# One core, a transformer block with a spectral filter, forward and backward: row stores and filter gradients issued by GpSimd, a column move on VectorE, four row statistics on ScalarE, and the queues written out anew

## The chip, the core and the metric

The kernel runs on one core of a Trainium2 chip. The core has five engines with a queue each: TensorE (PE in the profile; its weight loads are shown apart as PEld), VectorE (DVE), ScalarE (ACT), GpSimd (POOL) and SyncE (SP, which here only starts transfers). The metric is the time of one execution on the device in microseconds; the number given for a kernel is the median of its runs.

## The reference, cut to what matters

Inputs are bf16: x of 1x2048x512, a spectral filter w_r + i w_i of 2048x257, an MLP of width 1792 (w1, b1, w2, b2), a condition c of 1x512 and its matrix w_mod of 512x3072.

```python
def forward(x, w_r, w_i, w1, b1, w2, b2, c, w_mod):
    sa, ca, ga, sb, cb, gb = split6(silu(c) @ w_mod)
    h = layernorm(x) * (1 + ca) + sa
    x = x + ga * irfft2(rfft2(h) * (w_r + 1j * w_i))
    h = layernorm(x) * (1 + cb) + sb
    r = maximum(h @ w1 + b1, 0)
    return x + gb * ((r * r) @ w2 + b2)
```

The kernel returns this output (out_0) and, for a given grad_out, the gradients of all nine inputs: x (out_1), w_r and w_i (out_2, out_3), w1, b1, w2, b2 (out_4 to out_7), c (out_8) and w_mod (out_9).

## The kernel before, in words

**Tiling.** The 2048 rows lie as 16 tiles (NT) of 128 rows by 512 columns. The MLP takes them in four batches (NB) of four tiles, so 512 rows, and its 1792 columns in 14 pieces of 128 (NFC). The two-dimensional transforms are products with tables: the first stage over rows (spec_f1_half, "f1"), then for eight groups gi the second and third (spec_f23, "f2" and "f3"); spec_g1 and "g2", "g3" are the way to the other side. The backward pass runs through the same functions with the filter conjugated; it is called the way back here.

**Stages, in order of time.** (1) To about 15 us: the first loads; products of ones with themselves that nobody reads (L760, the warm-up products); silu(c); products with w_mod, among them column products mod_cols (L802) for gb2x, the factor 2 gb; transposes of w2, copied with that factor into w2T (L819); transposes of the first rows of grad_out into gT. (2) To about 47 us: statistics, norm and f1 for pairs of tiles (row_stats, row_norm), and the back products of the MLP, back_products (L912): for each batch and each of 14 pieces four products w2T x gT in one PSUM bank, copied to gaT by VectorE (one in five) or ScalarE. The banks of these products are the two buffers of "mm". In this stage the rest of the rows of mod (L789) and the bias row of the transform (psd, L891) are computed, too. (3) To about 79 us: the way there, spec_f23 then spec_g1. In spec_f23 one psB holds the second-stage product of a group, ScalarE copies it to AE (L359), a small TENSOR_TENSOR copies one column to the end of AE (L361, the column move), and f3 multiplies AE by the table LF; cmul multiplies by the filter on VectorE. (4) To about 100 us: g2 (L401), g3, residual, second norm. (5) From 100 to 256 us: the MLP, forward and back, by batches: products with w1 (L1086), squares on ScalarE (L1095), products with w2 and back. Here rows are stored to DRAM for later: h2_dram (L1041), gx1_dram (L1159), and the output out_0 (L1197). (6) From 256 to 305 us: the way back through spec_f23, with the products for the gradient of w1 (grad_w1, L1389) as other work for TensorE between the groups. After some groups, gm.emit computes a piece of the gradient of w_mod: a selection product (L488) with the matrix sel takes one row of grow to all 128 partitions, ScalarE copies it (gmbc, L490), and VectorE sums products with it into gsc (L500, with the tile gm_junk). The filter's gradients are left in the tiles Xb and go to out_2 and out_3 by strided stores (in ew_b). (7) To the end: spec_g1 of the way back, and the gradient of w2 (L1488) as other work beside the last sums of rows and the stores of out_1 (L1578).

**What sets the order.** The code is written in program order, and ORDER holds, for each engine, a list of numbers: instruction n is the n-th that the code emits for this engine, and the list is the order in which the engine's queue holds them. set_order chains each to the one before it with a dependency that orders only. So each queue runs in the order of its table; data dependencies still put waits into it. A change in the number of instructions shifts the numbers of all that come later, so numbers of two tables stand for the same instruction only after that shift.

```python
for name, runs in ORDER.items():
    ...
    for before, after in zip(seq, seq[1:]):
        tc.add_manual_dep(after, before.name, edge, reason="order")
```

## Time and profile before

| what | value |
|---|---|
| runs | 390.37, 390.41, 390.8 us; median 390.41 |
| the profiled execution | 391.62 us, span 389.8 us |
| granted TensorE clock, mean | 1.00 |
| moved by DMA | 89.75 MB, mean 230 GB/s |
| HBM | 39.23 MB read, 31.36 MB written |
| transfers started by hardware queue q1 | 131376 packets, 86.79 MB |
| transfers started by GpSimd (software queue q0) | 832 packets, 2.36 MB |

The span is the time from the first to the last recorded instruction of one execution on the chip, and the execution's own time stands beside it. The profile gives, for each engine, the time in which it executed instructions (starting a transfer is not counted), the same by stretches, and for a line of the kernel how often it ran, for how long, and how long the engine stood idle just before it and for whom. A row of the timeline is: start, duration, engine, line, operation, output<-input, shape, count, and in brackets the wait before it with the instruction that ended it. In a row by stretch the busy time of an engine has the number of its instructions in brackets; in a row by line three numbers with slashes are the shortest, the median and the longest duration in ns, then the first and last start.

### The profile page before, as it was taken

The page shows a single profiled execution, that of the slowest core. Times are in us where ns is not written, and L with a number is a line of the kernel's source. Part 1 is how long each engine was busy: PE and PEld are TensorE (multiplying, and loading weights), DVE is VectorE, ACT ScalarE, POOL GpSimd, SP SyncE. Part 2 cuts the span into 40 slices and gives each one's busy share as a digit, 9 for nine tenths or more (in the row PEclk, how much of TensorE's full clock was granted, in tenths as well). Part 3 has the DMA queues.
Part 4 walks back from the last instruction along what each step waited for, and adds up shares of the span by engine and source line. Part 5 has one row for each costly group of instructions (what it writes and reads, how often), then busy time and mean ns, then how long its engine had stood idle before and what let it go on. Part 6 is the DMA issues. An engine that isn't in the chain of part 4 may idle for free. (4 is left out here: it accounts for less than half of the span.)

```text
span 389.8 us, 8395 instructions
## 1 busy us (share of the span) xinstructions
PE 376.9 (97%) x3027; PEld 205.1 (53%) x3051; DVE 336.1 (86%) x823; ACT 303.9 (78%) x601; POOL 35.1 (9%) x117
## 2 busy tenths in 40 slices
PE   7999999989999999999999999999899999999996
PEld 2565677544444444444444445447678655444455
DVE  5999969959897479999999999992999976989975
ACT  4787999889888489859986998347476458889793
POOL 5652011000000000000000000010022000010111
DMA  8997989954696869559938899999899989999997
GB/s 273 366 250 201 227 157 229 307 177 176 202 241 154 215 163 183 124 122 281 305 77 176 204 265 190 284 266 314 216 273 321 257 216 298 207 288 223 255 297 231
DMA packets 132429, 89.75 MB, mean 230 GB/s; under 512 B 86974, under 2 KB 118212, under 8 KB 132132
## 3 DMA queue, kind: packets, MB, share of 16 engines
q1 hardware_dynamic: 131376, 86.79, 87.5%
q0 software_dynamic: 832, 2.36, 1.7%
q8 instruction: 24, 0.39, 0.4%
q14 instruction: 17, 0.14, 0.1%
q10 hardware_dynamic: 180, 0.07, 0.1%
HBM read 39.23 MB, written 31.36 MB: 181 GB/s over the span
## 5 line engine op out<-in xcount | busy, mean ns | idle before, releaser
L1389 PEld LDWEIGHTS <-h_sb 128*64 128x64 bf16 (+1 forms) x464 | 32.3, 109 | 14.7 <-issue 2.1
L1086 PEld LDWEIGHTS <-w 128*128 128x128 bf16 x224 | 21.3, 98 | 27.0 <-issue 3.0
L1389 PE MATMUL mm_0s<-gab,h_sb 128*64 128x384 bf16 (+2 forms) x288 | 35.0, 345 | 0.2 <-DMA h_sb<-h_dram 0.2
L1095 ACT ACTIVATE gab<-gab 128x512 bf16<-128x512 bf16 x56 | 34.8, 629 | 0.0
L1121 PEld LDWEIGHTS <-gab 128*128 128x128 bf16 x224 | 21.7, 98 | 24.7 <-ACT gab L1095 0.3
L912 PEld LDWEIGHTS <-w2T 128*128 128x128 bf16 (+1 forms) x280 | 24.2, 102 | 18.3 <-issue 3.8
L1488 PEld LDWEIGHTS <-gab 128*128 128x128 bf16 x192 | 18.6, 98 | 17.8 <-issue 1.4
L1121 PE MATMUL og_1s<-w1T,gab 128*128 128x512 bf16 x111 | 26.9, 379 | 0.1
L1121 PE MATMUL og_0s<-w1T,gab 128*128 128x512 bf16 x106 | 26.5, 379 | 0.2
L1389 PE MATMUL mm_1s<-gab,h_sb 128*64 128x512 bf16 (+2 forms) x176 | 23.7, 370 | 1.4 <-ACT gmbc L490 1.4
L1086 PE MATMUL mm_1s<-h2T,w 128*128 128x512 bf16 x84 | 23.2, 379 | 0.8 <-ACT gab L916 0.3
L1086 PE MATMUL mm_0s<-h2T,w 128*128 128x512 bf16 x80 | 21.9, 379 | 0.0
L1488 PE MATMUL mm_1s<-g_sb,gab 128*128 128x512 bf16 (+1 forms) x95 | 19.7, 352 | 0.4 <-DVE g_sb L1510 0.4
L1488 PE MATMUL mm_0s<-g_sb,gab 128*128 128x512 bf16 (+1 forms) x93 | 19.8, 352 | 0.1
L359 ACT ACTIVATE AE<-psB 128x1024 bf16<-128x1024 f32 x16 | 16.6, 1039 | 1.4 <-issue 1.2
L912 PE MATMUL mm_0s<-gT_0s,w2T 128*64 128x512 bf16 (+1 forms) x76 | 16.6, 380 | 0.6 <-DVE gab L914 0.5
L1086 PE MATMUL pst<-h2T,w 128*128 128x512 bf16 x60 | 16.9, 379 | 0.0
L912 PE MATMUL mm_0s<-gT_1s,w2T 128*128 128x512 bf16 (+1 forms) x64 | 16.0, 379 | 0.3
L912 PE MATMUL mm_1s<-gT_1s,w2T 128*128 128x512 bf16 (+1 forms) x68 | 16.1, 379 | 0.2
L912 PE MATMUL mm_1s<-gT_0s,w2T 128*128 128x512 bf16 (+1 forms) x72 | 15.8, 379 | 0.0
L321 POOL MEMSET AE<- 128x4 bf16 x4 | 0.5, 116 | 167.7 <-DVE h_6s L1089 167.7
L916 ACT CAST gab<-mm_1s 128x512 bf16<-128x512 f32 x24 | 14.3, 597 | 1.4 <-PE mm_1s L912 1.2
(619 smaller groups left out, 1045.3 us busy)
## 6 DMA issues: line engine op xcount, KB each, us to landing
w<-in_B_w_dram SPq DMA_DIRECT2D x2, 1792.0 KB, 7.1
Xb<-xs_dram SPq DMA_DIRECT2D x4, 514.0 KB, 6.2
Z<-wz_dram SPq DMA_DIRECT2D x4, 514.0 KB, 6.3
x_sb<-in_A_x_dram SPq DMA_DIRECT2D x4, 512.0 KB, 7.2
n_dram<-x_sb SPq DMA_DIRECT2D x4, 512.0 KB
h_dram<-h2r SPq DMA_DIRECT2D x8, 256.0 KB, 2.8
gx_dram<-n2rows SPq DMA_DIRECT2D x8, 256.0 KB, 5.1
h_sb<-h_dram SPq DMA_DIRECT2D x4, 512.0 KB, 4.7
```

Source lines behind the costliest of these rows:

```text
L321: nc.gpsimd.memset(ae[:, :, :, 256:257], 0.0)
L359: nc.scalar.activation(dst, ps.rearrange("p r b (e f) -> p (r b) f e", e=2), AF.Copy, scale=EF_S)
L912: nc.tensor.matmul(ps[m], lhsT=w2T[:, dc, fc * P + m.start:fc * P + m.stop], rhs=gT[b][:, :, dc, :], start=(dc == 0), stop=(dc == 3), **pos)
L916: nc.scalar.copy(out=gaT[b][:, fc, :], in_=ps)
L1086: nc.tensor.matmul(ps, lhsT=w1[:, dc, (fc + i) * P:(fc + i + 1) * P], rhs=h2T[b][:, :, dc, :], start=(dc == 0), stop=(dc == 3))
L1095: nc.scalar.activation(gh[:, i, :], gh[:, i, :], AF.Copy, accum_out=gb1[:, b, fc + i:fc + i + 1])
L1121: nc.tensor.matmul(ps, lhsT=lhs(fc), rhs=rhs[:, fc, :], start=(fc == 0), stop=(fc == NFC - 1))
L1389: nc.tensor.matmul(blocks(ps[m], fb), lhsT=h2_sb[:, t, dc * P + m.start:dc * P + m.stop], rhs=gh_rows(t, fb), start=(t == 0), stop=(t == N ...
L1488: nc.tensor.matmul(ps[:, 0:w], lhsT=h_rows(fc, t), rhs=g_sb[:, t, c:c + w], start=(t == 0), stop=(t == NT - 1))
```

## The change

**Fewer warm-up products.** 22 in place of 30. The four copies that spread silu(c) over columns (scb) become one copy with a broadcast input.

**Statistics.** For the tiles 4 to 7, row_stats_act computes mean and variance with two ScalarE passes a tile that sum while they write (a copy, and a square with the mean as bias), with small scalings on GpSimd, instead of VectorE's statistics instructions.

**Bias row.** psd, which had all 128 rows alike in 512 columns, becomes four 32-row strips of 128 columns each, computed in the four column tiles of the array; the first psB takes its bias by products per piece of 128 columns with the table ind, whose strips hold 1/32.

**Back products.** The transposes of w2 and grad_out use PSUM tiles declared as banks of 512 FP32 with a bf16 view, and the last five pieces of batch 0 and the first ten of batch 1 take turns over those two banks as well as the two of "mm". The release of three PSUM pools moves behind batch 1.

**Column move.** On the way back (dc is None) L361 runs on VectorE; on the way there it stays on GpSimd.

**Stores.** h2_dram (8), gx1_dram (8), out_0 (8) and the strided filter gradients of the groups 3 and 7 (24) are started by GpSimd, not SyncE.

**b1.** Its two copies run on ScalarE.

**Order.** All five tables of ORDER are new. The counts of instructions go from 3051 to 3045 (PE), 513 to 520 (ACT), 767 to 761 (DVE), 113 to 164 (POOL) and 299 to 251 (SP). Of the tables the diff shows here only the start of PE's and ACT's and the end of POOL's. In the new table of ACT, 20 to 23 and 26 to 29 are the statistics; in that of POOL, 131 to 142 are the stores of group 3, 124 to 129 those of group 0, 143 to 154 those of group 7, and 123 is the fill of the last row of sel.

```diff
...
                     extra = dc is not None and gi == 0 and hh == 0 and b == 0
-                    if extra:
-                        for cs in range(2):
-                            nc.tensor.matmul(ps[64 * cs:64 * cs + 64, hh, b, :], lhsT=dc[0], rhs=dc[1][:, 256 * cs:256 * cs + 256], start=True, stop=False,
-                                             tile_position=(0, 64 * cs))
                     for e in range(2):
...
                             c = 2 * e + cs
+                            if extra:
+                                nc.tensor.matmul(ps[64 * cs:64 * cs + 64, hh, b, P * e:P * e + P], lhsT=dc[0][:, c], rhs=dc[1], start=True, stop=False,
+                                                 tile_position=(0, 64 * cs))
                             nc.tensor.matmul(ps[64 * cs:64 * cs + 64, hh, b, P * e:P * e + P], lhsT=UT[:, c, 2 * (2 * gi + hh) + b, :, :],
-                                             rhs=K["Cd"][:, P * c:P * c + P], start=not extra, stop=(e == 1 if extra else True), tile_position=(0, 64 * cs))
+                                             rhs=K["Cd"][:, P * c:P * c + P], start=not extra, stop=True, tile_position=(0, 64 * cs))
             ae = AEs[gi % 2]
...
             end = ae.rearrange("p r b f -> p (r b) f")[64:P]
-            nc.gpsimd.tensor_tensor(end[:, :, 256::-256], end[:, :, 0:1].broadcast_to([64, 4, 2]), K["one0"][64:P, None, :].broadcast_to([64, 4, 2]), op=ALU.mult)
+            (nc.gpsimd if dc is not None else nc.vector).tensor_tensor(end[:, :, 256::-256], end[:, :, 0:1].broadcast_to([64, 4, 2]), K["one0"][64:P, None, :].broadcast_to([64, 4, 2]), op=ALU.mult)
             if gi > 0:
...
 ORDER = {
     "PE": (
-        "0 2 1 4 3 6 5 8 30 10 7 12 9 14 11 16 13 18 15 31 52 56 53 57-58 17 54 20 55 19 59 32-47 21-25 64-67 60-63 27 26 29 "
...
+        "0-3 5 4 7 6 9 11 22 8 13 15 17 44 10 23 12 48 24-38 45 39 46-47 49-50 14 19 51 21 16 52-59 18 20 68-75 60-67 40-43 "
...
     "ACT": (
-        "0 2 7 3 5 4 10 6 11-12 9 42 38 13-14 44 15 43 16 45 21 17 22 18 47 46 19-20 48-49 24 8 23 50 37 1 25 51-52 26-27 39 28 "
...
+        "0 2 4 20-21 3 7 22 8 23 9 26-27 6 28 47 10 48 11 49 12-13 29 18 14-15 50 16-17 51 19 43 55 24 52-53 56 25 80 54 42 30-31 "
+        "44 57 33 1 32 60 35 34 59 58 5 36-37 61 38 45 39 64 40-41 46 82 63 62 83 85 84 65 86 88 87 66 89-90 67 91 68 92 94 93 69 "
...
     "POOL": (
...
-        "89-90 97 99-101 95 102 96 103 92 91 93 88 94 104-105 111 107-108 110 109 112 106"
...
+        "45 68-69 77 48 43 15 75 36 35 76 71 78 72 47 33 9-10 59 4 73-74 46 49 8 52 79-80 60 81 5 55 50 13 51 14 11-12 82 56 2 54 "
+        "92 84-88 6 89-91 93-95 98-99 96-97 100-101 103-104 106 105 102 107 109 111 110 112 108 117 116 119 115 120 113 118 114 "
+        "121-122 130 136 142 129 127 123 134 132 124 128 140-141 139 135 131 126 137-138 133 125 149 152 145 143 154 150 144 148 "
+        "151 153 147 146 162 159 155-156 158 161 157 163 160"
     ),
...
     AEs = make_ae(nc, lfp)
-    dcrow = lfp.tile([P, D], BF16, name="dcrow")
-    ind = lfp.tile([P, NT, 4], BF16, name="ind")
-    nc.vector.memset(ind, 0.0)
-    nc.vector.memset(ind[0:1, :, 0:1], 1.0)
+    dcrow = lfp.tile([P, P], BF16, name="dcrow")
+    ind = lfp.tile([P, 4, NT, 4], BF16, name="ind")
+    nc.gpsimd.memset(ind, 0.0)
+    for k in range(4):
+        nc.gpsimd.memset(ind[32 * k:32 * k + 32, k, :, 0:1], 1.0 / 32)
     gen = Slots(tc, name="gen", bufs=1, side="right")
...
     sacol = p0.tile([P, 3, 4], BF16, name="sacol")
-    for k in range(30):
+    for k in range(22):
         ps = mmps.tile([P, 4, P], FP32, name="mm")
...
     nc.vector.tensor_tensor(sc, sigcol, ccolf, op=ALU.mult)
-    for dc in range(4):
-        nc.scalar.activation(scb[:, dc, :], ccolf[:, dc:dc + 1].broadcast_to([P, P]), AF.Copy, scale=sigcol[:, dc:dc + 1])
+    nc.scalar.copy(out=scb, in_=sc[:, :, None].broadcast_to([P, 4, P]))
     build_ta(tc, K, constp, gen, psM)
...
         a, z = W2H[h]
-        ps = psW.tile([P, 8, P], BF16, name="psW")
+        ps = psW.tile([P, D], FP32, name="psW").bitcast(BF16).rearrange("p (a q) -> p a q", a=8)
         for fc in range(a, z):
...
     def turn_g0(h):
-        ps = psW.tile([P, 2, 4, P], BF16, name="psW")
+        ps = psW.tile([P, D], FP32, name="psW").bitcast(BF16).rearrange("p (j c q) -> p j c q", j=2, c=4)
         for j in range(2):
...
 
+    def row_stats_act(t):
+        dev = p0.tile([P, 2], FP32, name="l1_dev", bufs=4)
+        nm = p0.tile([P, 2], FP32, name="l1_nm", bufs=4)
+        for j in range(2):
+            junk = p0.tile([P, D], BF16, name="l1_junk", bufs=2)
+            nc.scalar.activation(junk, x_sb[:, t + j, :], AF.Copy, accum_out=dev[:, j:j + 1])
+        nc.gpsimd.tensor_scalar(nm, dev, -1.0 / D, None, op0=ALU.mult)
+        for j in range(2):
+            junk = p0.tile([P, D], BF16, name="l1_junk", bufs=2)
+            nc.scalar.activation(junk, x_sb[:, t + j, :], AF.Square, bias=nm[:, j:j + 1], accum_out=dev[:, j:j + 1])
+        i1 = inv1[:, t:t + 2]
+        nc.gpsimd.tensor_scalar(dev, dev, 1.0 / D, None, op0=ALU.mult)
+        rstd(nc, i1, dev, K)
+        nbs[t] = p0.tile([P, 2], FP32, name="l1_nb", bufs=4)
+        nc.gpsimd.tensor_tensor(nbs[t], nm, i1, op=ALU.mult)
+
     def row_stats(t):
+        if t in (4, 6):
+            return row_stats_act(t)
         mv = p0.tile([P, 2, 2], FP32, name="l1_mv", bufs=4)
...
     pm = K["pm"]
-    psd = psM.tile([P, D], FP32, name="mod_ps", bufs=1)
-    for c, neg in enumerate(((), (1, 3), (1, 2), (2, 3))):
-        fs, co = slice(P * c, P * c + P), (0, 2, 1, 3)[c]
-        for i in range(4):
-            k = int(i in neg)
-            nc.tensor.matmul(psd[:, P * co:P * co + P], lhsT=sacol[:, k, i:i + 1].broadcast_to([P, P]), rhs=K["Cd"][:, fs], start=(i == 0), stop=(i == 3))
+    psd = psM.tile([P, D], FP32, name="mod_ps", bufs=1)[:, 0:P]
+    for i in range(4):
+        for k, neg in enumerate(((), (1, 3), (1, 2), (2, 3))):
+            nc.tensor.matmul(psd[32 * k:32 * k + 32, :], lhsT=sacol[:, int(i in neg), i:i + 1].broadcast_to([P, 32]), rhs=K["Cd"][:, P * k:P * k + P],
+                             start=(i == 0), stop=(i == 3), tile_position=(0, 32 * k))
     nc.vector.tensor_scalar(dcrow, psd, 128.0, None, op0=ALU.mult)
...
         nc.sync.dma_start(LF_dram[q], K["LFall"][:, q])
-    psW.release()
-    psM.release()
-    psF1.release()
-
 
-    def back_products(b):
+    def back_products(b, wide=()):
         for fc in range(NFC):
-            ps = mmps.tile([P, SB], FP32, name="mm")
+            k = (fc in wide and wide.index(fc)) % 4
+            ps = psW.tile([P, D], FP32, name="psW") if k > 1 else mmps.tile([P, SB], FP32, name="mm")
             for dc in range(4):
...
 
-    for b in range(NB - 1):
-        back_products(b)
+    back_products(0, range(9, NFC))
+    back_products(1, range(10))
+    psW.release()
+    psM.release()
+    psF1.release()
+    back_products(2)
     p0.release()
...
 
-        spec_f23(tc, K, UT, AEs, (ind.rearrange("p a b -> p (a b)"), dcrow), dest_f, ew_f)
+        spec_f23(tc, K, UT, AEs, (ind.rearrange("p c a b -> p c (a b)"), dcrow), dest_f, ew_f)
     lfp.release()
...
                 nc.vector.tensor_tensor(h2r, h2r, modb[:, SB_B, None, :].broadcast_to([P, 2, D]), op=ALU.add)
-                nc.sync.dma_start(h2_dram[t // 4, :, t % 4:t % 4 + 2, :], h2r)
+                nc.gpsimd.dma_start(h2_dram[t // 4, :, t % 4:t % 4 + 2, :], h2r)
                 if b > 0:
...
                 nc.vector.tensor_tensor(gx1, gx1, v, op=ALU.add)
-                nc.sync.dma_start(gx1_dram[t // 2], gx1)
+                nc.gpsimd.dma_start(gx1_dram[t // 2], gx1)
                 if ub is not None:
...
                 nc.vector.tensor_tensor(x1, o, x1, op=ALU.add)
-                nc.sync.dma_start(out0_view[:, t:t + 2, :], x1)
+                nc.gpsimd.dma_start(out0_view[:, t:t + 2, :], x1)
                 sums(t)
...
             nc.vector.tensor_tensor(gb1[:, 0, :], gb1[:, 0, :], gb1[:, k + 1, :], op=ALU.add)
-        nc.vector.tensor_copy(b4[:, 0:NFC], gb1[:, 0, :])
+        nc.scalar.copy(out=b4[:, 0:NFC], in_=gb1[:, 0, :])
         ps = mmps.tile([P, P], BF16, name="mm")
...
         b4r = gmp.tile([NFC, P], BF16, name="b4r", bufs=1)
-        nc.vector.tensor_copy(b4r, ps[0:NFC, :])
+        nc.scalar.copy(out=b4r, in_=ps[0:NFC, :])
         nc.sync.dma_start(out_5.rearrange("(fc p) -> fc p", p=P), b4r)
...
                     for b in range(2):
-                        K["gW"] = nc.sync.dma_start(v[:, b, :, a:a + n, :].rearrange("u h g f -> u h (g f)"),
+                        K["gW"] = nc.gpsimd.dma_start(v[:, b, :, a:a + n, :].rearrange("u h g f -> u h (g f)"),
                                                     X[64 * b:64 * b + 32].rearrange("u h g f -> u h (g f)")).ins
                         for h in range(2):
-                            K["gW"] = nc.sync.dma_start(v[:, 1 - b, 1 - h, 16 - a:16 - a - n:-1, :], X[64 * b + 32:64 * b + 64, h]).ins
+                            K["gW"] = nc.gpsimd.dma_start(v[:, 1 - b, 1 - h, 16 - a:16 - a - n:-1, :], X[64 * b + 32:64 * b + 64, h]).ins
 
```

174 rows, old and new, of the table ORDER are left out of this document.

## The prediction

> **What bounds the kernel now.** I read the page first, then the busy time by stretches, then TensorE's timeline wherever it stands idle.
>
> ```profile
> span 389.8 us, 8395 instructions
> PE 376.9 (97%) x3027; PEld 205.1 (53%) x3051; DVE 336.1 (86%) x823; ACT 303.9 (78%) x601; POOL 35.1 (9%) x117
> ```
>
> ```profile
> 8.40:14.80 6.40, 5.84 (x64) 3.72 (x66) 6.37 (x29) 3.96 (x9) 3.92 (x16) 1.00 1.06 368
> 14.80:50.00 35.20, 34.37 (x295) 20.60 (x295) 34.23 (x127) 30.91 (x51) 11.56 (x35) 1.00 0.93 246
> 50.00:78.00 28.00, 27.74 (x441) 19.74 (x437) 24.45 (x53) 26.16 (x46) 2.70 (x7) 1.00 0.99 230
> 78.00:101.00 23.00, 21.05 (x172) 10.77 (x170) 17.61 (x43) 21.68 (x43) 0.00 (x0) 1.00 0.45 150
> 101.00:256.00 155.00, 153.58 (x775) 70.27 (x789) 138.32 (x294) 124.48 (x276) 0.12 (x1) 1.00 0.84 202
> 256.00:305.00 49.00, 47.38 (x600) 34.73 (x598) 41.33 (x96) 30.02 (x51) 7.97 (x21) 1.00 1.05 284
> ```
>
> The columns are the stretch, its length, the busy time of PE, PEld, DVE, ACT and POOL, the clock, the DMA share and GB/s. TensorE is the bound: from 14.8 us on it is idle for hundredths of its time in every stretch but 78 to 101, where it lacks 23.00 - 21.05 = 1.95 us. So an edit gains only by taking work from TensorE, by letting its first useful work start earlier, or by closing a hole; work moved between the other engines gains nothing unless TensorE waits for them. The second thing to see is how close the others are: VectorE is full from 8.4 to 50 us (6.37 of 6.40, 34.23 of 35.20), and ScalarE lacks only 1.84 us of 28.00 from 50 to 78 us.
>
> **The change, part by part.** The sum is made against the profiled span, 389.8 us. That execution took 391.62 us, and the median of the runs is 390.41, so I carry differences of the span over to 390.41.
>
> *Eight warm-up products fewer.* First the way to the first useful long product.
>
> ```profile
> 5.75 0.63 PE L760 MATMUL mm_0s<-ones_sq 128*128 128x512 bf16 x1
> 6.18 0.44 PE L760 MATMUL mm_1s<-ones_sq 128*128 128x512 bf16 x1
> 6.45 0.38 PE L760 MATMUL mm_0s<-ones_sq 128*128 128x512 bf16 x1
> 6.67 0.38 PE L760 MATMUL mm_1s<-ones_sq 128*128 128x512 bf16 x1
> ...
> 7.54 0.38 PE L760 MATMUL mm_1s<-ones_sq 128*128 128x512 bf16 x1
> 8.89 0.23 PE L128 MATMUL sm_ps<-ident,TA 128*128 128x128 bf16 x1 [0.97 <-ACT TA L124]
> ...
> 10.05 0.54 PE L802 MATMUL sm_ps<-sacol,wm_2s 128*128 128x1 bf16 x16
> 10.86 0.15 DVE L807 TENSOR_SCALAR gb2x<-sm_ps 128x4 f32<-128x4 f32 x1
> 11.05 0.69 ACT L819 ACTIVATE w2T<-psW_0s,gb2x 128x512 bf16<-128x512 bf16 x1 [1.34 <-DVE gb2x L807]
> 14.59 0.38 PE L760 MATMUL mm_0s<-ones_sq 128*128 128x512 bf16 x1
> 14.80 1.03 PE L912 MATMUL mm_1s<-gT_0s,w2T 128*128 128x512 bf16 x4
> ```
>
> Warm products follow each other by 0.22 us (6.45 to 6.67), so eight are worth 8 x 0.22 = 1.7 us if TensorE had something else to do. It mostly has not: before 14.80 the chain is the column products (10.05), gb2x (10.86), two rounds of scaled copies (the first at 11.05), the transposes of the gradient and their copies. Counted in the two order tables, 21 warm-ups stand ahead of the column products now and 16 afterwards, so these can come up to 5 x 0.22 = 1.1 us earlier. I take 0.5 us, because gb2x also has its place in the full VectorE queue. Against it stands ScalarE's queue: the squares of rows 4 and 5 now stand between the two scaled copies and the copy of gT_0, 0.1 us late each by the gaps there. Net -0.3 us; ends -1.1 and +0.5.
>
> *The bias row on four column tiles.* L891 is 16 full products one after the other; L789 shows sixteen 32-column products, four at a time.
>
> ```profile
> L891 PE MATMUL mod_ps<-Cd,sacol 128*128 128x128 bf16 x16 | 1.4, 219 | 0.0
> 29.90:31.10 1.20, 1.05 (x16) 0.33 (x16) 1.00 0.82 180
> ...
> 69.54 1.04 PE L912 MATMUL mm_1s<-gT_0s,w2T 128*128 128x512 bf16 x4
> 70.51 0.40 PE L385 MATMUL psG_1s<-LG,Z 64*128 64x128 bf16 x12
> ```
>
> The second row is L789: 1.05 us for four passes of 512 columns, each about 0.22 us plus one tail. At 128 columns a pass is a quarter, so L891 goes from 16 x 0.055 = 0.88 us of array time to 4 x 0.055 = 0.22: -0.66 us. The other two rows price a change between the whole array and tiles: the last of four products starts at 69.54 + 3 x 0.22 = 70.20 and the next would follow at 70.42, not 70.51, so about 0.1 us a change. I count 67 such changes in the old order and 70 in the new: +0.3 us. The bias products of the first psB (two of 256 columns become four of 128) are the same array time. Net -0.4 us; ends -0.7 and 0.
>
> *Holes.* Four banks instead of two for the back products of parts of batches 0 and 1, and a new order of every queue.
>
> ```profile
> 30.63 0.38 PE L789 MATMUL mod_ps<-wm_1s,gab 128*32 128x512 bf16 x1
> 31.55 0.38 PE L912 MATMUL mm_0s<-gT_0s,w2T 128*128 128x512 bf16 x1 [0.54 <-DVE gab L914]
> ...
> 82.36 0.38 PE L401 MATMUL psT<-Cf,utcs 128*128 128x128 bf16 x4 [0.47 <-ACT Tsb_1s L403]
> 86.43 0.38 PE L401 MATMUL psT<-Cf,utcs 128*128 128x128 bf16 x4 [0.39 <-ACT Tsb_0s L403]
> ...
> 272.65 0.39 PE L488 MATMUL mm_1s<-grow,sel 128*128 128x512 bf16 x1
> 278.01 0.41 PE L1389 MATMUL mm_1s<-gab,h_sb 128*64 128x512 bf16 x2 [1.37 <-ACT gmbc L490]
> ```
>
> The wait at 31.55 is for a bank, which two more banks answer: -0.5. Between 82 and 87 us the new order puts single back products between the column products that wait for Tsb, where the old one has runs of several: of the 1.95 us I take a third, -0.6. At 278 us a bank waits for a copy that waits for VectorE's sums of the earlier gradient of w_mod; the first selection product stands 46 places earlier on TensorE, so its sums can be done earlier: half, -0.7. New holes must be expected where three queues are rewritten that are all nearly full: +0.5. Net -1.3; ends: all three holes closed (-3.9), or none and 1.5 us of new ones.
>
> *Four statistics on ScalarE.* Eight reads of 128x512 with a sum replace four statistics and four aggregations.
>
> ```profile
> L1095 ACT ACTIVATE gab<-gab x56: 612/620/675, 110.2 to 234.7; 128x512 bf16<-128x512 bf16 x56
> L1095 ACT ACTIVATION_READ_ACCUMULATOR gab<-gab x56: 185/191/245, 110.7 to 235.3; 128x1 f32 x56
> L768 ACT ACTIVATE gab<-ccolf,sigcol x4: 384/384/390, 8.7 to 11.6; 128x128 bf16<-128x128 f32 x4
> L837 DVE BATCH_NORM_STATS2 l_st_1s<-x_sb x4: 675/680/695, 5.1 to 32.3; 128x6 f32<-128x512 bf16 x4
> L838 DVE BATCH_NORM_AGGREGATE l_mv_1s<-l_st_2s x2: 164/165/166, 7.4 to 23.6; 128x2 f32<-128x6 f32 x2
> ```
>
> VectorE loses 4 x (0.68 + 0.17) = 3.4 us where it is full. ScalarE gets 8 x 0.62 to 8 x 0.81 = 5.0 to 6.5 us, and loses four copies of 0.38 for one wide copy of some 0.6: +4.0 to +5.6, say 4.6. Its idle time from 8.4 to 50 us is 2.44 + 4.29 = 6.7 us, so it is covered: 0. Without that cover, 4.6 us.
>
> *Stores on POOL, the column move, b1.* 48 stores leave SP's queue.
>
> ```profile
> L361 POOL TENSOR_TENSOR AE<-AE,one 64x8 bf16<-64x8 bf16 x16 | 5.9, 372 | 54.6 <-ACT AE L359 54.6
> L500 DVE SCALAR_TENSOR_TENSOR gm_junk<-wmc_0s,onef,gmbc x8: 739/742/750, 272.3 to 298.8; 128x512 bf16<-128x512 bf16 x8
> L1440 POOL DMA_DIRECT2D out_dram<-Xb x6: 549/564/787, 287.6 to 299.8; - x6
> L1041 SPq DMA_DIRECT2D h_dram<-h2r x8: 337/506/835, 101.0 to 216.6; - x8
> 293.33 0.42 DVE L446 TENSOR_TENSOR Xb<-p 128x514 bf16<-128x514 bf16 x1
> 299.89 0.39 PE L488 MATMUL mm_1s<-grow,sel 128*128 128x512 bf16 x1
> ```
>
> A store holds POOL for 0.55 to 0.79 us (the L1440 row): 48 x 0.56 = 27 us, on an engine with 0.12 us of work from 101 to 256 us. SP is freed of 48 x 0.5 = 24 us of issuing; no long wait of TensorE hangs on SP, so the gain is 0 (ends 0 and -0.5). Eight column moves of 0.37 us on POOL become VectorE's, between 0.17 us (the aggregation, the nearest small row) and 0.37; VectorE has 7.7 us free from 256 to 305, and other products fill TensorE behind the move: 0, ends -0.3 and +0.5, since it now queues behind a product of 0.7 us. b1's two copies are two short instructions on ScalarE: 0. What waits behind the stores on POOL is one small fill: the last row of the selection matrix stands behind two filter stores of group 3 and two of group 0 in the new order. Group 3 is written at 293.75; four stores of 0.56 and a fill of 0.2 end at 296.2, and TensorE needs it at 299.89, less the 2.0 us by which all may come earlier, so 297.9: covered.
>
> The longest of the six L1440 stores, all beside a busy VectorE, took 0.79 us. The Trainium skill (SBUF — State Buffer, section "A bandwidth-pool intuition that's wrong (but worth ruling out)") says a DMA issued from GpSimd waits, with its descriptors unwritten, until a VectorE instruction in a two-port mode ends, 620 ns becoming about 3100. Those six stores do not show it; by its figure the four stores would take 12.4 us and the fill would be 8 us late.
>
> Sum: -0.3 - 0.4 - 1.3 = -2.0 us; 390.41 - 2.0 = **388.4 us**.
>
> **Rivals.**
>
> *ScalarE becomes the bound before 78 us.* Place: its queue from 14.8 to 50 us. Its idle time there, 4.29 us, is made of waits for TensorE; if none of it can be used, only the 2.44 us before 14.8 take up the added 4.6, the first AE copies come 2.2 us late, and 50 to 78 us with 1.84 us free cannot make it up. Then the gains before 78 us are lost, and -0.6 - 0.7 remain: +0.9 us, 391.3; with new holes 391.8. It decides when less than half of the 4.29 us is usable. For it speaks that ScalarE copies four in five back products; against it, that VectorE, full there, is relieved by 3.4 us.
>
> *The holes move.* The order closes as much as it opens; only the array time is saved, -0.4, and the start is eaten by the squares: 390.0.
>
> *POOL's stores wait for VectorE.* If a store waits out one VectorE instruction (0.75), four take 5.2 us, the fill ends at 299.2 and TensorE loses 1.3 us: 389.7. It decides from 1.0 us a store. The rule named above from the Trainium skill is this mechanism; no store of the L1440 row is that long.
>
> *The array's clock falls back.* Up to 6.18 us products follow by 0.43 us, then by 0.22, though the clock column shows 1.00 throughout. With fewer warm-ups and waits between 7 and 13 us the slow pace could return for as long as at first, 1.07 to 6.18: half of 5.1 us, +2.5, so 390.9. Against it: the hole of 7.54 to 8.89 us did not bring it back. The Trainium skill (TensorE: Matmul & The Clock Gate, section "Part 1: The HAM clock gate (the "warmup" mystery)") puts the fall after an idle window of about 3.4 us; the trace's shorter hole agrees.
>
> *More is closed.* All of the warm-ups (-1.7), the array time (-0.4) and two thirds of the holes (-2.6 + 0.5): 386.2.
>
> **How the numbers follow.** What a measurement here can tell from no change is about 0.2%, 0.8 us. Chances: forecast 0.57 (its own range 387.0 to 389.6), more closed 0.09, holes move 0.15, POOL 0.04, clock 0.03, ScalarE 0.12. Faster: 0.57 + 0.09 = 0.66; within: 0.15 + 0.04 + 0.03 = 0.22; slower 0.12. The range reaches to the near edge of the fullest gain and into ScalarE's case: 386.6 to 391.2.
>
> **What would show it.** Right: the first L912 product before 14.6 us; L891 busy about 0.4 us; no wait of 0.5 us near 31 us; less than 1.95 us idle between the first L401 and the first L1086; the wait for gmbc L490 below 1 us; POOL stores of 0.55 to 0.8 us. Wrong: the first AE copy later than now relative to TensorE's order with ScalarE solid before it (ScalarE's case); stores over 1 us with TensorE waiting for sel (POOL's); products 0.43 us apart after 8 us (the clock's).

## The result, and the profile after

The changed kernel takes 402.11 us in the median (401.0 to 406.46) against 390.39 us for the kernel before: a ratio of 1.033 with a 95% interval of 1.024 to 1.041, so 11.7 us slower where 2.0 us faster was forecast. A median counts every execution; a ratio compares means and leaves out the three executions that took over 1.5% longer than the fastest of their kernel (398.83 and 782.49 us with all stores but h2, 2200.14 us of the kernel before). The profiled execution is the fastest of the four: 401.0 us, span 399.2 us. Lines of the changed kernel have numbers 15 to 19 higher than before in most places (the back products are L927, L912 before), those inside the functions of the transforms one lower.

The page of the changed kernel: the span, then the busy time of the engines.

```profile
span 399.2 us, 8441 instructions
PE 375.8 (94%) x3022; PEld 201.3 (50%) x3045; DVE 333.7 (84%) x817; ACT 307.1 (77%) x616; POOL 60.1 (15%) x168
```

TensorE works 1.1 us less than before (375.8 against 376.9) and is idle 10.5 us more (399.2 - 375.8 = 23.4 against 389.8 - 376.9 = 12.9). So the 9.4 us of span are new holes in TensorE, not work. The busy time by the same stretches as before (length, then PE, PEld, DVE, ACT, POOL, clock, DMA share, GB/s) says where they lie.

```profile
8.40:14.80 6.40, 5.40 (x59) 3.25 (x60) 5.87 (x25) 6.08 (x14) 4.21 (x19) 1.00 1.07 375
14.80:50.00 35.20, 33.77 (x292) 19.41 (x291) 32.10 (x120) 32.81 (x60) 14.30 (x46) 1.00 1.00 243
50.00:78.00 28.00, 26.41 (x436) 19.56 (x432) 23.41 (x53) 24.90 (x43) 2.03 (x8) 1.00 0.88 220
78.00:101.00 23.00, 20.41 (x178) 10.50 (x173) 15.75 (x38) 20.09 (x39) 0.00 (x0) 1.00 1.00 230
101.00:256.00 155.00, 153.28 (x766) 69.00 (x779) 138.62 (x297) 124.14 (x278) 11.07 (x20) 1.00 0.81 188
256.00:305.00 49.00, 44.58 (x552) 30.72 (x551) 36.64 (x89) 29.25 (x49) 5.17 (x14) 1.00 1.00 269
```

The largest losses are 2.8 us between 256 and 305 us (47.38 busy before) and 1.3 us between 50 and 78 us (27.74 before). VectorE and ScalarE have room in both. The view of TensorE's waits (who waited for whom: us in total, times, longest) and the timeline name them.

```profile
PE mm_0s L1408 <- DMA h_sb<-h_dram: 3.5, 1, 3.5
PE psT L400 <- ACT Tsb_0s L402: 2.3, 1, 2.3
PE mm_1s L1507 <- DVE g_sb L1529: 1.5, 1, 1.5
...
PE mm_0s L927 <- DVE gab L929: 1.2, 1, 1.2
...
PE psC_1s L338 <- DVE AE L360: 0.7, 1, 0.7
...
PE mm_1s L1408 <- ACT gmbc L489: 0.2, 1, 0.2
```

```profile
14.80 0.82 PE L927 MATMUL mm_0s<-gT_0s,w2T 128*128 128x512 bf16 x3
...
74.83 1.20 SPq L962 DMA_DIRECT2D xs_dram<-Xs_1s  x1
76.07 0.71 SPq L1123 DMA_DIRECT2D wz_dram<-in_A_w_i_dram  x1
78.84 4.54 SPq L1244 DMA_TRANSPOSE w1T<-in_B_w_dram  x1
83.97 0.60 ACT L402 ACTIVATE Tsb_0s<-psT 128x512 bf16<-128x512 f32 x1 [2.30 <-DMA wz_dram<-in_A_w_i_dram]
84.62 0.38 PE L400 MATMUL psT<-Cf,utcs 128*128 128x128 bf16 x4 [2.27 <-ACT Tsb_0s L402]
...
260.60 0.61 SPq L1283 DMA_DIRECT2D h_sb<-h_dram  x1
266.07 1.05 PE L1408 MATMUL mm_0s<-gab,h_sb 128*64 128x512 bf16 x8 [3.48 <-DMA h_sb<-h_dram]
```

The two longest holes end with transfers that SyncE starts: the copy Tsb at 83.97 waits for a transfer issued at 76.07, behind the store of Xs_1s, and the products for w1's gradient wait 3.48 us for the last load of h2_sb, issued at 260.60. The same two instructions of SyncE's queue in the kernel before:

```profile
60.39 0.52 SPq L943 DMA_DIRECT2D xs_dram<-Xs_1s  x1
...
253.75 0.87 SPq L1264 DMA_DIRECT2D h_sb<-h_dram  x1
```

They stand 14 and 7 us earlier there. That is SyncE's new table, not the moved stores themselves. The third wait shown, 1.2 us for VectorE's copy to gab, stands at 61.70 us; no single wait of 0.5 us or more lay between 50 and 78 us before.

Part of the time is not holes. The four executions had a mean granted clock of 0.998, 0.982, 0.995 and 0.991; span x (1 - clock) is 0.8, 7.3, 2.0 and 3.6 us, and without it the four are 400.2, 399.2, 399.2 and 399.4 us. In the profiled execution, though, the 0.8 us lie behind TensorE's last product: the clock is 1.00 up to 396 us and falls to 0.50 only after that, so its 401.0 us hold nothing of it. The median of +11.7 us is then +9 to +10.6 us at full clock and 1 to 3 us of a clock that fell for a while. The same reckoning is used below as "at full clock". It is an estimate: the clock is given to three digits (0.4 us), and a fall behind the last product, up to 0.9 us in the traces, is counted with the rest.

### The profile page after: what moved, and what is told of

It reads as the page before. It is cut to its first block, busy times and chain, and to the rows that moved or that the text cites. A ratio compares the mean times of both kernels' runs of the same rounds, so it can differ in the third digit from the quotient of the medians.

```text
span 399.2 us, 8441 instructions
## 1 busy us (share of the span) xinstructions
PE 375.8 (94%) x3022; PEld 201.3 (50%) x3045; DVE 333.7 (84%) x817; ACT 307.1 (77%) x616; POOL 60.1 (15%) x168
## 5 line engine op out<-in xcount | busy, mean ns | idle before, releaser
L1408 PEld LDWEIGHTS <-h_sb 128*64 128x64 bf16 (+1 forms) x464 | 31.1, 108 | 18.3 <-DMA h_sb<-h_dram 4.0
L1408 PE MATMUL mm_0s<-gab,h_sb 128*64 128x384 bf16 (+2 forms) x288 | 32.9, 345 | 3.6 <-DMA h_sb<-h_dram 3.5
L927 PEld LDWEIGHTS <-w2T 128*128 128x128 bf16 (+1 forms) x280 | 24.1, 102 | 17.4 <-issue 3.3
L1408 PE MATMUL mm_1s<-gab,h_sb 128*64 128x512 bf16 (+2 forms) x176 | 22.7, 370 | 0.2 <-ACT gmbc L489 0.2
L1507 PE MATMUL mm_0s<-g_sb,gab 128*128 128x512 bf16 (+1 forms) x93 | 20.7, 352 | 0.2
L1060 POOL DMA_DIRECT2D h_dram<-h2r x8 | 4.6, 580 | 84.8 <-DVE h2r L1059 38.3
L927 PE MATMUL mm_0s<-gT_0s,w2T 128*64 128x512 bf16 (+1 forms) x72 | 15.4, 380 | 1.4 <-DVE gab L929 1.2
L400 PEld LDWEIGHTS <-utcs 128*128 128x128 bf16 x128 | 10.3, 97 | 12.6 <-issue 5.5
L927 PE MATMUL mm_1s<-gT_1s,w2T 128*128 128x512 bf16 (+1 forms) x60 | 15.0, 380 | 0.0
L927 PE MATMUL mm_1s<-gT_0s,w2T 128*128 128x512 bf16 (+1 forms) x68 | 14.9, 380 | 0.0
L1468 POOL DMA_DIRECT2D out_dram<-Xb x16 | 8.8, 555 | 40.2 <-DVE Xb L445 33.9
## 6 DMA issues: line engine op xcount, KB each, us to landing
w<-in_B_w_dram SPq DMA_DIRECT2D x2, 1792.0 KB, 10.5
```

The costliest lines, as they stand in the source:

```text
L400: nc.tensor.matmul(ps[:, P * i:P * i + P], lhsT=CS[:, i, t].rearrange("p a b -> p (a b)"), rhs=K["Cf"][:, i, :], start=True, stop=True)
L927: nc.tensor.matmul(ps[m], lhsT=w2T[:, dc, fc * P + m.start:fc * P + m.stop], rhs=gT[b][:, :, dc, :], start=(dc == 0), stop=(dc == 3), **pos)
L1060: nc.gpsimd.dma_start(h2_dram[t // 4, :, t % 4:t % 4 + 2, :], h2r)
L1408: nc.tensor.matmul(blocks(ps[m], fb), lhsT=h2_sb[:, t, dc * P + m.start:dc * P + m.stop], rhs=gh_rows(t, fb), start=(t == 0), stop=(t == N ...
L1468: K["gW"] = nc.gpsimd.dma_start(v[:, 1 - b, 1 - h, 16 - a:16 - a - n:-1, :], X[64 * b + 32:64 * b + 64, h]).ins
L1507: nc.tensor.matmul(ps[:, 0:w], lhsT=h_rows(fc, t), rhs=g_sb[:, t, c:c + w], start=(t == 0), stop=(t == NT - 1))
```

## The experiments

The expectations name their theories by letters. P: stores that GpSimd starts land later and hold what others wait for. O: the new order of SyncE's own transfers costs. C: the new order of the compute queues costs. G: with fewer warm-up products the clock falls. H: of the stores, the eight of h2_dram carry the largest part, through the single buffer h2r. Besides, the edits to the arrays and the statistics may each cost by themselves. Each ratio is to the kernel before, run on the same chip.

### The 48 stores alone, in the old order

```diff
-                nc.sync.dma_start(h2_dram[t // 4, :, t % 4:t % 4 + 2, :], h2r)
+                nc.gpsimd.dma_start(h2_dram[t // 4, :, t % 4:t % 4 + 2, :], h2r)
-                nc.sync.dma_start(gx1_dram[t // 2], gx1)
+                nc.gpsimd.dma_start(gx1_dram[t // 2], gx1)
-                nc.sync.dma_start(out0_view[:, t:t + 2, :], x1)
+                nc.gpsimd.dma_start(out0_view[:, t:t + 2, :], x1)
...
-                        K["gW"] = nc.sync.dma_start(v[:, b, :, a:a + n, :].rearrange("u h g f -> u h (g f)"),
+                        K["gW"] = nc.gpsimd.dma_start(v[:, b, :, a:a + n, :].rearrange("u h g f -> u h (g f)"),
```

The kernel before with these lines (and the mirrored filter stores), everything else in the old order.

> The kernel before with one part of the change: the 48 stores (8 of h2_dram, 8 of gx1_dram, 8 of out_0, 24 of the filter gradients) start on GpSimd, each put in GpSimd's queue at the time at which SyncE started it; the rest of SyncE's queue and the other queues keep their order. Theory O (the loss comes from the new order of SyncE's transfers): no change, 389.5 to 391.5 us. Theory P (stores from GpSimd land later and hold buffers and lanes that loads wait for): 396 to 402 us. Theory C (the loss comes from the new order of the compute queues): no change, 389.5 to 391.5 us.

Measured: 399.29 us, 1.024 [1.019, 1.029]: 9 us slower without any other edit. Its timeline, then the same stretch of SyncE's queue in the kernel before:

```profile
100.37 7.76 SPq L1228 DMA_TRANSPOSE w1T<-in_B_w_dram  x1
...
111.49 5.28 SPq L1228 DMA_TRANSPOSE w1T<-in_B_w_dram  x1
111.91 0.55 POOL L1044 DMA_DIRECT2D h_dram<-h2r  x1 [9.41 <-DVE h2r L1043]
120.29 0.69 DVE L1042 TENSOR_TENSOR h2r<-n2rows,modb 128x1024 bf16<-128x1024 bf16 x1 [2.39 <-DMA h_dram<-h2r]
134.73 1.04 PE L1089 MATMUL mm_1s<-h2T,w 128*128 128x512 bf16 x4 [2.86 <-DMA h2T<-h2r]
```

```profile
101.00 0.83 SPq L1041 DMA_DIRECT2D h_dram<-h2r  x1
101.88 5.73 SPq L1225 DMA_TRANSPOSE w1T<-in_B_w_dram  x1
...
111.52 0.34 SPq L1041 DMA_DIRECT2D h_dram<-h2r  x1
112.88 4.38 SPq L1225 DMA_TRANSPOSE w1T<-in_B_w_dram  x1
```

Before, each store stood ahead of a transpose of w1 on one queue. With the stores gone from it, the transposes start at once (100.37 for 101.88, 111.49 for 112.88), and the store issued at 111.91 lands only at 120.2, 8.3 us later (before, the one issued at 111.52 took 2.8). h2r has one buffer, so VectorE's next h2 rows wait 2.39 us for it, and the first transpose from h2r to h2T starts at 122.39 us, not at 121.23. That is 1.2 of the 3.5 us by which the products come later (134.73 for 131.27); the next section shows where the rest comes from. TensorE waits 2.86 us. Then the clock falls; the same stretches of this kernel (PE busy first, the clock the third figure from the end):

```profile
132.00:134.00 2.00, 0.00 (x0) 0.00 (x0) 0.99 (x2) 0.98 (x2) 0.00 (x0) 1.00 1.00 266
134.00:136.00 2.00, 1.27 (x6) 0.61 (x7) 2.00 (x5) 0.13 (x1) 0.00 (x0) 0.94 1.22 285
136.00:138.00 2.00, 2.00 (x6) 0.64 (x5) 0.42 (x3) 1.14 (x3) 0.00 (x0) 0.50 0.52 191
138.00:140.00 2.00, 1.95 (x7) 0.84 (x7) 0.47 (x1) 1.50 (x5) 0.00 (x0) 0.71 0.00 0
```

The lost clock is 2 x (0.06 + 0.50 + 0.29) = 1.7 us on top of the hole.

### Which of the stores: all but h2, h2 alone, the rows, the filter

```diff
-                nc.sync.dma_start(h2_dram[t // 4, :, t % 4:t % 4 + 2, :], h2r)
+                nc.gpsimd.dma_start(h2_dram[t // 4, :, t % 4:t % 4 + 2, :], h2r)
```

The second kernel below has only this edit (8 stores). The first has the other 40 stores on GpSimd and not this one, the third the three kinds of rows (24 stores), the fourth the filter's gradients (24 stores); all in the old order.

> The kernel before with 40 of the 48 stores on GpSimd: the eight of h2_dram stay on SyncE. Theory H (the largest loss of the run with all 48 comes from h2r, which has one buffer: a store of it landed 8.3 us after its start, the next h2r and the transposes to h2T came late, and the hole of 2.86 us at 132 us cost a fall of the clock of 1.7 us on top): 394 to 396 us, no hole above 1 us at 130 to 136 us, no fall of the clock there. If the loss is spread over all stores: 397.5 to 399 us.

> The kernel before with only the eight stores of h2_dram on GpSimd, each at its old time. Theory H (these eight carry the largest part, through the single h2r buffer): 393 to 396 us, with the hole at 132 us. If the loss needs all the stores together: 390 to 391.5 us.

> The kernel before with the 24 row stores (h2_dram, gx1_dram, out_0) on GpSimd, each at its old time; the filter gradients stay on SyncE. Theory H: 395 to 398 us. If the filter gradients are what costs (small strided stores that go beside the load of g_sb, and the last row of sel filled late behind them): 390 to 392 us.

> The kernel before with the 24 stores of the filter gradients on GpSimd, each at its old time. Theory H: 391 to 392.5 us, with a wait for sel of about 1 us at 300 us. If the filter gradients carry the loss: 395 to 398 us.

Measured: all but h2 395.42 us, 1.011 [1.007, 1.014]; h2 alone 398.07, 1.021 [1.017, 1.025]; rows 396.21, 1.016 [1.012, 1.020]; filter 392.13, 1.006 [1.003, 1.009]. TensorE's waits with h2 alone, then with the filter alone:

```profile
PE mm_0s L1089 <- DMA h2T<-h2r: 3.1, 1, 3.1
PE mm_1s L1089 <- DMA h2T<-h2r: 3.0, 1, 3.0
...
PE pst L1089 <- DMA h2T<-h2r: 1.1, 1, 1.1
```

```profile
PE mm_1s L1491 <- DVE g_sb L1513: 2.2, 1, 2.2
```

The ranges that theory H gave held for three of the four; h2 alone lost more than its 393 to 396 us.

Eight stores are enough for a loss of 8 us, with 7.2 us of waits for h2T. From the second batch on, SyncE transposes two h2r a batch to h2T, and each is stored as well. The third batch's second h2r, with h2 alone on GpSimd, then with all 48 stores there:

```profile
213.98 1.26 SPq L1048 DMA_TRANSPOSE h2T<-h2r  x1
214.25 0.54 POOL L1044 DMA_DIRECT2D h_dram<-h2r  x1 [5.18 <-DVE h2r L1043]
220.74 0.82 PE L1089 MATMUL mm_0s<-h2T,w 128*128 128x512 bf16 x3 [3.08 <-DMA h2T<-h2r]
```

```profile
214.70 1.25 SPq L1048 DMA_TRANSPOSE h2T<-h2r  x1
218.18 0.82 PE L1089 MATMUL mm_0s<-h2T,w 128*128 128x512 bf16 x3
221.83 0.54 POOL L1044 DMA_DIRECT2D h_dram<-h2r  x1
```

With h2 alone GpSimd's queue holds nothing else there, so the store starts 0.27 us behind the transpose of the same rows, and the products come 6.8 us behind the transpose; with other stores ahead of it in the queue it comes 7.1 us behind the transpose, and the products start after 3.5 us (3.6 in the kernel before, where SyncE issued this store at 216.58). VectorE did not wait for h2r there, so this hole is not one of the single buffer. Of the nine second transposes in the runs with 48 stores, 24 rows and h2 alone, five have a store 0.3 us behind them, and these five are the holes of over 1 us (2.86; 2.26; 2.99, 1.10 and 3.08); the four with the store 7 to 8 us behind have none. This also says why eight stores alone cost more than the same eight among 24. It is read from where the stores stand; no run moved this store alone.

The waits of 3.1 and 3.0 us are longer than the 2.86 above, and yet the clock did not fall behind them in this execution. The filter's stores cost about 2 us; where, isn't shown. In their trace TensorE waits 2.2 us for VectorE's product with the load of grad_out (g_sb; 0.4 us before), but that wait is 0.4 us with all 48 stores and 1.2 us with the warm-up products alone. The parts do not add up (8 us for h2 alone, 4 for all the others, 9 together).

### The changed kernel with the stores back, and with two transfers moved up

The first puts the 48 stores back on SyncE at the places that answer to their old ones. The second leaves them on GpSimd and moves two instructions in SyncE's table: 48 is the store of Xs_1s, 153 the last load of h2_sb.

```diff
- ... 45 49 ... 47-48 ... 152 139 118 149 80 153 156-157 ...
+ ... 45 48-49 ... 47 ... 152-153 139 118 149 80 156-157 ...
```

> The changed kernel with its 48 stores back on SyncE, each at the place in SyncE's new queue that answers to the time at which GpSimd started it; all else stands as in the change. Theory P (stores started by GpSimd land later, and what waits for their buffers is late; 9 us in the old order): 391 to 396 us. Theory O (the new order of SyncE's own transfers is what costs): 399 to 403 us.

> The changed kernel with two transfers moved up in SyncE's queue and nothing else: the store of Xs_1s, ready at 60 us, from 74.8 us to behind the store of Xs_0s at 60.4 us, and the last load of h2_sb from 260.6 us to behind the one at 252.8 us. Theory O: the holes of 2.27 us at 82 us and 3.48 us at 263 us go, 395 to 398 us. Theory P: the holes come from GpSimd's stores, so 400 to 403 us.

Measured: stores back 398.04 us, 1.018 [1.014, 1.023], 394.6 to 395.4 at full clock; two moved up 398.34, 1.022 [1.015, 1.029], 395.0 to 397.5 at full clock. So the stores cost about 4 us in the new order, and the places of two transfers as much, 3 us of it at full clock; there the ranges lie apart (395.0 to 397.5 against 399.2 and more), while the intervals of the ratios overlap. Waits with the stores back, then with the two moved up:

```profile
PE mm_0s L1410 <- DMA h_sb<-h_dram: 3.4, 1, 3.4
PE psT L400 <- ACT Tsb_0s L402: 1.7, 1, 1.7
```

```profile
PE mm_1s L1509 <- DVE g_sb L1531: 3.5, 1, 3.5
PE mm_0s L1410 <- DMA gab<-gab: 2.6, 1, 2.6
```

With the stores back, the waits for the two late transfers stay and g_sb's goes; with the transfers early, Tsb's hole is gone, the load's hole is handed on to another transfer (3.48 to 2.59 us), and g_sb's grows. P and O each hold for a part, in different places; both measured times lie between the two theories' ranges. In the new order the h2 stores open no hole of their own, and TensorE is busy 153.28 of 155 us in the MLP: three of the four transposes of w1 now start between 78.84 and 91.39 us, ahead of these stores, and the second store of a batch comes some 16 us or more behind its transpose (129.73 and 145.62 in the first such batch). That these transposes crowd the transfer that Tsb waits for is likely from the timeline, but no run moved them alone.

### Both, with the old number of warm-up products; and this without the column move

```diff
-    for k in range(22):
+    for k in range(30):
...
-                nc.gpsimd.dma_start(h2_dram[t // 4, :, t % 4:t % 4 + 2, :], h2r)
+                nc.sync.dma_start(h2_dram[t // 4, :, t % 4:t % 4 + 2, :], h2r)
```

The changed kernel with the stores back, the two transfers moved up, and 30 warm-up products. The second kernel below undoes the column move and b1's copies in it as well.

> The changed kernel with three things undone at once: the stores back on SyncE (4 us by its own run), the store of Xs_1s and the last load of h2_sb moved up in SyncE's queue (3.8 us by its own run), and eight more warm-up products from 12.3 us on. If the gains add up: 393 to 395 us; if the stores and the moves are two cures of one wait: 396 to 398 us.

> The mended kernel of the run before (stores on SyncE, two transfers moved up, 30 warm-up products; 395.2 us) with the column move of the way back on GpSimd and b1's copies on VectorE again; in the new order. If the column move costs in the new order what it costs in the old one (1.9 us): 393 to 394 us, and what is left against the kernel before (some 3 us) lies in the statistics, the bias row, the banks and the new order itself. If it costs nothing here: 395 to 396 us.

Measured: 395.19 us, 1.014 [1.010, 1.018], at full clock 393.1 to 394.8; and 395.5, 1.012 [1.005, 1.019]. Of the 11.7 us 7 are undone by the three edits together. The two kernels cannot be told apart; the second one's interval is 5 us wide, so a cost of the column move like that in the old order is not excluded. The 30 warm-up products do not keep the clock up: in both traces it is at half from about 11 to 15 us, as in the first kernel's row for 12 to 14 us (the clock again third from the end).

```profile
12.00:14.00 2.00, 1.94 (x11) 1.07 (x10) 1.40 (x3) 1.50 (x5) 0.12 (x1) 0.50 1.10 351
```

In the first, TensorE still waits 1.9 us for gab, 1.5 for Xb and 1.4 for the back products' banks.

### The new order without its stores' order, and the edits without the new order

The first two keep the changed kernel but give SyncE's queue the order of before (with the stores on GpSimd, then with them back on SyncE). The third has all edits and the old order on every engine.

```diff
-    "SP": (  (the new table)
+    "SP": (  (the table of before, its numbers shifted)
```

> The changed kernel with one table set back: the 251 transfers that are left to SyncE stand in the order that they had before; GpSimd still starts its 48 stores. Theory O: the waits for h_sb (3.5 us), for the Tsb of the first g2 (2.3 us) and for g_sb (1.5 us) go, so 392 to 396 us. Theory P: no better than 400 us. Theory C: no better than 399 us.

> The changed kernel with the 48 stores back on SyncE, whose whole queue is that of before; the compute queues are those of the change. Theory O: 392 to 396 us, like the run with the stores still on GpSimd. Theory P: 391 to 394 us, and several us faster than that run. Theory C: 399 to 402 us.

> All edits of the change, but every queue in the order of before; new instructions stand where those stood that they replace. Theory O: 388.5 to 391 us. Theory P: 396 to 402 us. Theory C: 388.5 to 391 us. If the edits themselves cost (statistics on ScalarE, a late column move), it is above 391 us with the loss before 80 us or between 256 and 305 us.

Measured: 424.21 us, 1.088 [1.084, 1.093]; 424.97, 1.090 [1.084, 1.095]; 408.73, 1.045 [1.041, 1.050]. In the second, TensorE waits once for 4.5 us (a copy of ScalarE's), once for 4.1 (h2T) and once for 3.9 (w2T).

The first two decide nothing between the theories: a table of transfers made for one order of the products makes holes of 4 us in another, whoever starts the stores. They show only that the tables belong together. The third says more. Without any new table the edits together lose 18 us (about 12 at full clock), where O and C gave no loss and P at most 402 us; so the new order is not needed for a loss.

### Single edits in the old order

22 warm-up products alone; the bias row and the four banks; the four statistics (with the single copy of scb); the column move and b1's copies; and all of these but the statistics.

```diff
-    for k in range(30):
+    for k in range(22):
```

> The kernel before with the last eight of its 30 warm-up products left out (those from 10.4 to 14.4 us) and nothing else. By the prediction's term: 390.1 us, ends 389.3 and 390.9. Theory G (with fewer warm-up products between 9 and 14.4 us TensorE's granted clock falls to one half for some 3.4 us, as it did in the run of the array edits at 13 to 17 us): +1.7 us, so 391.5 to 392.3 us, and a fall of the clock between 11 and 18 us in the profile.

```diff
-    psd = psM.tile([P, D], FP32, name="mod_ps", bufs=1)
+    psd = psM.tile([P, D], FP32, name="mod_ps", bufs=1)[:, 0:P]
...
-    def back_products(b):
+    def back_products(b, wide=()):
```

> The kernel before with the bias row on four column tiles and the back products on four banks, nothing else. By the prediction's terms (-0.4 and -0.5): 389.5 us, the wait of 0.54 us at 31 us gone. Theory G says nothing here. If the gain is eaten by what stands behind it: 390.0 to 390.8 us.

```diff
     def row_stats(t):
+        if t in (4, 6):
+            return row_stats_act(t)
```

> The kernel before with the statistics of tiles 4 to 7 on ScalarE and the one copy for scb; ScalarE's new instructions stand behind the same neighbours as in the change, the rest in the old order. By the prediction's term: no change, 390 to 391 us. If ScalarE's idle time before 50 us does not cover them: up to 395 us, with the first copy to gaT and the first AE copy late.

```diff
-            nc.gpsimd.tensor_tensor(end[:, :, 256::-256], end[:, :, 0:1].broadcast_to([64, 4, 2]), K["one0"][64:P, None, :].broadcast_to([64, 4, 2]), op=ALU.mult)
+            (nc.gpsimd if dc is not None else nc.vector).tensor_tensor(end[:, :, 256::-256], end[:, :, 0:1].broadcast_to([64, 4, 2]), K["one0"][64:P, None, :].broadcast_to([64, 4, 2]), op=ALU.mult)
...
-        nc.vector.tensor_copy(b4r, ps[0:NFC, :])
+        nc.scalar.copy(out=b4r, in_=ps[0:NFC, :])
```

> The kernel before with the column move of the way back on VectorE and b1's copies on ScalarE, nothing else. By the prediction's terms: 390.1 us, ends 389.8 and 390.6. If the move, queued behind VectorE's products of 0.7 us, is what f3 waits for (0.7 us in one wait of the changed kernel): 391 to 392.5 us.

```diff
-    for k in range(30):
+    for k in range(22):
...
-    for dc in range(4):
-        nc.scalar.activation(scb[:, dc, :], ccolf[:, dc:dc + 1].broadcast_to([P, P]), AF.Copy, scale=sigcol[:, dc:dc + 1])
+    nc.scalar.copy(out=scb, in_=sc[:, :, None].broadcast_to([P, 4, P]))
...
```

> The kernel before with all parts of the change but the stores and the statistics: 22 warm-up products, the one copy for scb, the bias row on four column tiles, back products on four banks, the column move on VectorE, b1 on ScalarE; all queues in the old order. By the prediction's terms (-0.3, -0.4, -0.5): 389.2 us; if the fewer warm-up products or the column move cost, 391 to 393 us. Theories P and O say nothing else here.

| edit | us | ratio [95%] |
|---|---|---|
| warm-up products | 391.48 | 1.0037 [1.0011, 1.0064] |
| bias row and banks | 391.69 | 1.0041 [1.0015, 1.0067] |
| statistics | 392.24 | 1.0064 [1.0035, 1.0093] |
| column move, b1 | 391.96 | 1.0045 [1.0021, 1.0068] |
| all but the statistics | 394.51 | 1.0103 [1.0068, 1.0137] |

None gains; the first four lose 1.4 to 2.5 us each, by the ratios. A wait with the warm-up products alone, one with the statistics alone, and a stretch of the last kernel:

```profile
PE psW_1s L817 <- DVE w2T L820: 0.9, 1, 0.9
```

```profile
PE mm_0s L932 <- DVE gab L934: 1.4, 1, 1.4
```

```profile
14.00:16.00 2.00, 1.78 (x9) 0.90 (x8) 1.72 (x10) 0.89 (x1) 0.48 (x4) 0.50 1.07 359
```

Time that the warm-up products leave free becomes waiting: the wait of 0.9 us for w2T is there with 22 of them alone and in the last kernel, and in no old-order kernel with 30. With the statistics, the back product at 33.20 us waits longer for VectorE's copy, 1.4 us for 0.5. In the last kernel the clock is at half from about 13 to 17 us, though not in all its executions: three of four had a mean clock of 1.000, as had eleven of the twelve with 22 warm-up products alone. The profile with the warm-up products alone has no fall before its last product. So theory G is not shown as the cause of that single edit's loss. The executions of the kernel before themselves spread over 388.3 to 392.9 us, so one trace can't place a loss of 1.5 us.

No version was faster than the kernel before. Two direct tests were not made: a second buffer for h2r, and GpSimd's second h2 store held back until its transpose has landed.

## Why the prediction was wrong

**The bound: right.** TensorE's time decides; +10.5 us idle and -1.1 us busy are the whole of the span's +9.4.

**Stores: the step that failed.** "48 stores leave SP's queue ... no long wait of TensorE hangs on SP, so the gain is 0", and "What waits behind the stores on POOL is one small fill". The cost of issuing was right: a store held POOL for 0.54 to 0.81 us. Two things were not in the sum. One is what a store runs beside, how long it then takes to land, and who waits. From issue to landing the eight stores of h2r took, before and after (shortest, median, longest):

```profile
DMA to landing us min/median/max: 2.3/2.8/7.7
```

```profile
DMA to landing us min/median/max: 3.2/4.3/6.3
```

The 7.7 us are SyncE's own, for the store at 101.00 just ahead of a transpose of w1. So a store beside such a transpose landed late with either engine, and what GpSimd changes is the company: of the six h2r that are transposed, SyncE's old table kept five stores 1.3 us or more behind their transpose, while a store on GpSimd starts as soon as its rows are written and nothing stands ahead of it. The other thing is what moves up in the queue that the stores leave: transposes of 4 to 8 us. The sum had the stores' place in that queue as issue time only. In the old order this is 8 us from eight stores; in the new order the stores are worth 4 us, which the traces place only in part: the wait for g_sb is 1.5 us with them on GpSimd and gone with them back, but 1.8 us again in the last mended kernel, where they are on SyncE too.

**The new order: mis-sized.** New holes were put at +0.5 us, from three queues "that are all nearly full". SyncE's table had no term in the sum. It holds two transfers that stand 14 and 7 us later, worth 3 to 4 us.

**Holes.** The one at 31.55 us went, as forecast, but a wait of 1.2 us for the same kind of copy stands at 61.70. That at 278 us went from 1.4 to 0.2 us, but in kernels that don't touch it the same wait is 0.5 us (the 48 stores, h2's alone), 0.6 (the warm-up products) or 1.8 (the rows' stores): it changes with whatever shifts the queues, so -0.7 was no gain of this edit. Between 82 and 87 us, instead of -0.6 us, there is a hole of 2.27.

**Warm-up products.** The column products came 0.3 us earlier (9.79 for 10.05), not 0.5. The first long back product starts at 14.80 us in both, so -0.3 was 0 at that place, and alone the edit costs 1.4 us (0.4 to 2.5 by the interval), beyond the upper end of +0.5.

**Bias row.** The groups by line (L891 before):

```profile
L908 PE MATMUL mod_ps<-Cd,sacol 128*32 128x128 bf16 x16 | 0.4, 222 | 0.0
```

The products fell from 1.4 to 0.4 us of busy time, more than the 0.66 worked out, and the time didn't follow: with the banks +1.6 us.

**Statistics and ScalarE's rival.** "So it is covered: 0" held at its own place: in the changed kernel the first AE copy comes at 48.0 us, 0.3 us later than before, not 2.2. But alone, in the old order, the edit costs 2.5 us, and the longest new wait in its trace is for a copy of VectorE's (1.4 us), the engine that it relieves.

**Column move.** Near the lower bound of 0.17 us given, and TensorE waited once for it, 0.7 us:

```profile
L360 DVE TENSOR_TENSOR AE<-AE,one x8: 191/192/195, 272.3 to 306.9; 64x8 bf16<-64x8 bf16 x8
```

With b1's copies it costs 1.8 us in the old order, and nothing that could be measured in the mended new one, whose interval could hide as much.

**The rivals.** POOL's had the right change and the wrong wait: the fill of sel delayed TensorE in the old order, by up to 1.1 us, and not in the changed kernel's trace. No store held GpSimd as if it waited out a VectorE instruction there. The rule of the Trainium skill weighed in the prediction (SBUF — State Buffer, section "A bandwidth-pool intuition that's wrong (but worth ruling out)"; 620 ns becoming about 3100) is not borne out as the prediction used it: 0.81 us at most. The clock's rival is real: by the mean clocks it takes some 2 to 7 us of three of the changed kernel's executions. Its one trace has no fall before the last product, so the place in the others isn't shown; with the stores back, in the same order of the products, it fell from about 11 to 15 us, where the rival had put it. A fall is to 0.50 for 3.4 us and costs 1.7 us, or lasts twice as long. The argument against the rival, that a hole of 1.35 us did not bring the slow pace back, does not carry: that fall came behind holes of 1.05 and 0.81 us. Nor is the rule of the Trainium skill cited there (TensorE: Matmul & The Clock Gate, section "Part 1: The HAM clock gate (the "warmup" mystery)"), a fall after an idle window of about 3.4 us, borne out as a bound on one hole: with the 48 stores and with the two transfers moved up a fall came behind holes of 2.86 and 2.59 us. "The holes move" is nearest in kind: they moved, and grew.

**What stays open.** The mended version is still 5 us slower than the kernel before, some 3 of it at full clock. The statistics, the bias row, the banks and the new tables are in it; which of them, the runs don't say.

## What to carry to other kernels

Moving a transfer to another engine's queue is a change to both queues: ask what now starts earlier in the queue it left, what the moved transfer now runs beside, above all a transfer that reads the same tile, how long both take to land then, and which buffer is held until then; a single buffer makes the landing time a price. Read the table of the transfers as closely as that of the busiest engine, since a queue on which nobody waits may owe that only to its order. Check every hole that a gain is to come from in more than one execution.

## What the runs showed of the hardware

A 256 KB store started by GpSimd took 4.3 us in the median to land where SyncE's took 2.8, and up to 8.3 us beside a transpose of w1 that held SyncE for 5.3. SyncE's own took 7.7 us ahead of a transpose of w1 that held it for 5.7. A transpose from h2r to h2T landed 3.1 to 3.2 us after its issue, and after 4.0 to 5.1 us with GpSimd's store of the same h2r starting 0.1 to 0.3 us behind it.

The granted clock fell to 0.50 after a hole of 2.86 us in one kernel and not after holes of 2.99, 3.08 and 3.48 us in others; behind a hole of 3.35 us (the stores back) it stayed there for 6.8 us, not 3.4. Between 10 and 22 us it fell in the traces of six kernels with 22 warm-up products and of the two mended ones with 30, not in those of the changed kernel and of 22 alone; and in the same kernel, not in each execution. The Trainium skill (TensorE: Matmul & The Clock Gate, section "Part 1: The HAM clock gate (the "warmup" mystery)") says that a free-running window of about 3.4 us decides, so that the slow part varies from run to run; the falls here, at half clock for 3.4 us or twice that and not tied to the length of a hole, agree.
